# Loads of the rearranged Wo issued later, in a sliding-window attention block with a parallel gated MLP

## The chip, the cores and the metric

The kernel runs on one core of one Trainium2 chip. A core has a matrix engine (TensorE, PE in the profile; its weight loads stand apart as PEld), a vector engine (VectorE, DVE), a scalar engine (ScalarE, ACT), GpSimd (POOL) and SyncE (SP). In this kernel SP issues nearly all DMA transfers; 16 DMA engines carry them out. Each engine works through its own instructions in program order and waits on semaphores for the others. The metric is the device time of one execution in microseconds, lower is better. A run's time is the median over its executions; one more execution is recorded by the profiler, and all views of the profile are of that one.

## The reference

One layer for one prompt of S = 2048 positions of width D = 640: a layer norm, and from it, in parallel, a causal attention with a window of 256 positions (32 heads of 20) and a gated MLP of width 1536. All inputs are bfloat16.

```python
xn = layernorm(x)
qkv = xn @ wqkv                                # -> q, k, v: 32 heads of 20
scores = q @ k.T * 20 ** -0.5                  # per head
scores = where(0 <= i - j < 256, scores, -1e9)
attn = softmax(scores) @ v                     # heads side by side: 2048 x 640
g, u = xn @ w_gate, xn @ w_up
out = x + attn @ wo + (sigmoid(g) * u) @ w_down
```

## The kernel before

The positions are cut into four chunks of 512 (c = 0 to 3), each of four blocks of 128 rows. For each chunk TensorE computes q and k (`proj_block`, L266), v (`both_v`, L324; in chunk 0 L304), the twelve GLU blocks (`g_gu`: gate at L414, up at L423), the scores (`scores`, L500), the products with v (`pv`, L533) and the output (`g_out`). Around a GLU block ScalarE takes the tanh (L417) and VectorE makes h (L427). ScalarE takes the exponential of the scores (L506); GpSimd (L489) and VectorE (L517) set what lies outside the window to zero.

The output of a block of 128 rows is two PSUM tiles of 320 columns. In each, `down` (L437) sums h times w_down over 12 parts, and then `add_wo` (L444) adds attn times Wo over 5 parts. VectorE adds x, which lies in a tile `rows` (L448), and SP stores the result (L459). The rows of x are loaded by `new_rows` (L454), two blocks ahead at the start of `g_out`.

**Order.** The kernel is scheduled by hand: the order in which the program issues operations is the order on each engine. The main loop (L759) goes through steps of scores. Into the time of each step it pulls pieces of other work from a list, `fill`, whose parts stand in a fixed order (L726 to L745) with a cost in ns. A part with cost 0 is a group of DMA issues (`later`). The parts around the change are, in order: q and k of chunk 1 (`qk1`), the loads of w_down (`wd`), v of chunk 1 (`v1`), the rest of q and k of chunk 1 (`rest1`, issued by SP at L287), the loads of Wo (`wo`), the last three GLU blocks of chunk 0 (`gu0c`), the first two GLU blocks of chunk 1 (`gu1a`), and the output of chunk 0 with the third GLU block of chunk 1 inside its first block (`out0`). Beside `gu0c` and `gu1a` VectorE normalizes chunk 2 and turns it (`norm_block` L227, `turn_block` L244); when the last of four turns is done, SP writes it to DRAM (`turn_rows`, L249) and reads it back as xnT of chunk 2 (L251).

**Wo.** The rows of Wo are needed in another order than they have in DRAM. Eight DMAs that GpSimd issues beside q and k of chunk 1 (`turn_wo`, L179) write them in that order to a DRAM buffer `wo_i`. `load_wo` (L182) then loads them from there into the tile `wo`, 128 partitions of 5 x 640: four DMAs issued by SP, 32 partitions each, 200 KB each, in rows of 1280 bytes. The tile is written once and read in the outputs of all four chunks. A read of a tile waits for every write to the part that it reads, and a write for the writes of the same part before it.

In `g_out` the order of chunk 0 is: issue the two first `rows` loads; `down` for both halves of the first 128 rows; the third GLU block of chunk 1; then `add_wo` for both halves (the first use of Wo), `add_x`, and the store.

Of the kernel before, what the change touches and what calls it, by code (L numbers as in the profile page):

```python
# [69 lines left out]
def kernel(  # L70
# [11 lines left out]
    nc = tc.nc  # L82
# [42 lines left out]
    wo = const.tile([P, DC, D], BF16, name="wo")  # L125
# [54 lines left out]
                            in_=rows[r, side].rearrange("i (e w) -> e i w", e=16))  # L180

    def load_wo():  # L182
        for i in range(HG):
            nc.sync.dma_start(out=wo[32 * i:32 * i + 32, :, :],
                              in_=wo_i[i].rearrange("(m j) n -> j m n", j=32))
# [192 lines left out]
    def g_qk(c, behind={}):  # L378
        for w in "qk":
            for m in range(DC):  # L380
                proj_block(w, c, m)
                behind.get((w, m), lambda: None)()
                yield 5 * MM
        if c:
            spread("q", c, 0, 2)
            spread("k", c, 0, 2)
        else:
            for r in range(2):
                spread("q", c, r, r + 1)
                spread("k", c, r, r + 1)  # L390
                if r == 0:
                    load_gu(wu, B_w_up, 0, FS // 2)
# [13 lines left out]
    def part(w, d, f):  # L406
        k, first = divmod(f * P, FS)
        return w[k][:, d, first:first + P]

    def g_gu(c, f0, f1):  # L410
        for f in range(f0, f1):
            pg = ps_d.tile([P, CW], FP32, name="pg", tag="d")
            for d in range(DC):
                nc.tensor.matmul(pg, lhsT=part(wg, d, f), rhs=xnT[c][:, :, d, :],  # L414
                                 start=(d == 0), stop=(d == DC - 1))
            th = tp.tile([P, CW], FP32, name="th")
            nc.scalar.activation(out=th, in_=pg, func=TANH, scale=0.5)  # L417
            fill.hold = True
            yield 5 * MM
            fill.hold = False  # L420
            pu = ps_d.tile([P, CW], FP32, name="pu", tag="d")
            for d in range(DC):
                nc.tensor.matmul(pu, lhsT=part(wu, d, f), rhs=xnT[c][:, :, d, :],  # L423
                                 start=(d == 0), stop=(d == DC - 1))
            h = hp.tile([P, CW], BF16, name="h")
            ht[c, f] = h
            nc.vector.scalar_tensor_tensor(out=h, in0=th, scalar=1.0, in1=pu, op0=ADD, op1=MULT)  # L427
            yield 5 * MM
# [6 lines left out]
    def down(c, s, y, cut):  # L435
        for f in range(FC):
            nc.tensor.matmul(y[:, 0:cut[1] - cut[0]], lhsT=ht[c, f][:, s * P:(s + 1) * P],  # L437
                             rhs=wd[:, f, cut[0]:cut[1]], start=(f == 0), stop=False)
            if f % 6 == 5:
                yield 6 * 136  # L440
# [11 lines left out]
    def new_rows(c, s, name="rows", bufs=3, queue=nc.sync):  # L452
        rows = lnp.tile([P, D], BF16, name=name, bufs=bufs)
        queue.dma_start(out=rows, in_=xr[:, c * SBC + s, :])  # L454
        return rows
# [5 lines left out]
    def outp(c, s, ys, rows):  # L461
        for y, cut in zip(ys, HALVES):
            add_wo(c, s, y, cut)
        for y, cut in zip(ys, HALVES):
            add_x(y, cut, rows)
        store(c, s, rows)

    def g_out(c, between, ahead=()):
        coming = new_rows(c, 0)
        for s in range(SBC):  # L470
            rows = coming
            if s < SBC - 1:
                coming = new_rows(c, s + 1)
            if s == 0:
                yield from ahead
            ys = [ps_d.tile([P, CW], FP32, name=f"y{i}", tag="d") for i in range(2)]
            for y, cut in zip(ys, HALVES):
                yield from down(c, s, y, cut)
            if s == 0:
                yield from between  # L480
                fill.flush()
            outp(c, s, ys, rows)
            yield 10 * 136
# [128 lines left out]
    def mix(a, b, first, every=1, rest=True):  # L612

        for k, cost in enumerate(a):
            yield cost
            if k >= first and (k - first) % every == 0:
                yield next(b, 0)
        if rest:
            yield from b
# [94 lines left out]
    fill = Fill()  # L714
# [3 lines left out]
    def later(load, *args):  # L718
        load(*args)
        yield 0  # L720
# [8 lines left out]
    fill.add("wd", later(load_wd), 0)  # L729
    fill.add("v1", mix(g_v(1), norms2, 2, 1, False), 40 * 136)  # L730
    fill.add("rest1", later(spread_rest, 1), 0)
    fill.add("wo", later(load_wo), 0)
    fill.add("gu0c", mix(g_gu(0, 9, 12), norms2, 0, 1, False), 3 * GU)
    fill.add("gu1a", mix(g_gu(1, 0, 2), norms2, 0, 1, False), 2 * GU)
    fill.add("out0", mix(g_out(0, g_gu(1, 2, 3)), norms2, 1, 1), OUT + GU)
    fill.add("qk2", mix(g_qk(2), norms3, 2, 1, False), 50 * MM)
    fill.add("v2", g_v(2), 40 * 136)
# [108 lines left out]
```

## Time and profile before

| | us |
|---|---|
| median of 3 runs | 308.88 |
| lowest and highest of them | 308.87, 311.01 |
| the profiled execution, its own time | 309.65 |
| its span, from the first to the last instruction | 308.0 |
| ScalarE busy, VectorE busy | 193.2, 184.4 |
| GpSimd busy | 83.8 |

The span is 1.65 us shorter than the profiled execution's time; the rest lies around the program's instructions. The profiled execution is 0.77 us above the median. The granted clock of TensorE is 1.000 over the span.

DMA traffic is uneven. The page's 40 slices are 7.7 us each; their DMA share is 0.7 or more in most of the first eleven and lower, with peaks, after that:

```profile
DMA  7997739889927222721152113550000210000301
GB/s 213 347 306 238 266 102 309 220 248 320 198 94 199 85 72 93 228 80 47 43 128 72 39 65 99 163 192 2 3 2 2 70 41 23 2 2 2 88 21 64
```

The first line gives the mean busy share of the 16 DMA engines in tenths, the second what they moved. Two issues of Wo's neighbourhood, from the page's list (destination and source, queue, count, KB each, median us from issue to landing):

```profile
rows<-in_A_x_dram SPq DMA_DIRECT2D x12, 160.0 KB, 3.5
...
wo<-wo_i SPq DMA_DIRECT2D x4, 200.0 KB, 9.1
```

A landing time counts from the issue, so it holds the wait behind transfers that were issued before, as well as the transfer.

### The profile page before, as it was taken

Reading aid. Unit: us, or ns where it says so; the run is one execution under the profiler, and the core shown is the slowest. Engines: PE = TensorE matmul, PEld = TensorE weight load, DVE = VectorE, ACT = ScalarE, POOL = GpSimd, SP = SyncE. Lnnn points to the kernel's source line nnn. Section 1 sums busy time; section 2 is a strip of 40 time slices with the busy share of each in tenths; the row PEclk is TensorE's granted clock in tenths of the full one; section 3 lists DMA queues with packets and bytes.
Section 4 is the critical chain, followed back from the end, with each engine's and each line's share of the span. In section 5 each row is a group of like instructions: output and inputs, shape, how many; then the busy total and the mean of one; then the engine's idle time right before and its main releaser. Section 6 shows DMA issues by size and latency. Waiting matters only on the chain.

```text
span 308.0 us, 10147 instructions
## 1 busy us (share of the span) xinstructions
PE 302.9 (98%) x4431; PEld 168.2 (55%) x4431; DVE 184.4 (60%) x378; ACT 193.2 (63%) x183; POOL 83.8 (27%) x189
## 2 busy tenths in 40 slices
PE   7999999999999999999999999999999999999996
PEld 3654445564456655654456655644546765444774
DVE  5787449298984579577642666454383627465523
ACT  6923785977766458867655557777766466778000
POOL 5011234635314133422213122241314132221100
PEclk9999999999999999999999999999999999999999
DMA  7997739889927222721152113550000210000301
GB/s 213 347 306 238 266 102 309 220 248 320 198 94 199 85 72 93 228 80 47 43 128 72 39 65 99 163 192 2 3 2 2 70 41 23 2 2 2 88 21 64
DMA packets 35756, 36.86 MB, mean 120 GB/s; under 512 B 2944, under 2 KB 35456, under 8 KB 35712
## 3 DMA queue, kind: packets, MB, share of 16 engines
q1 hardware_dynamic: 34304, 33.84, 36.6%
q0 software_dynamic: 544, 1.61, 1.7%
q10 hardware_dynamic: 864, 0.77, 0.9%
q8 instruction: 34, 0.56, 0.8%
q14 instruction: 10, 0.08, 0.1%
HBM read 25.59 MB, written 11.44 MB: 120 GB/s over the span
## 4 chain that ended last, share of the span: by engine, by line
PE 97%; DMA 1%; ACT 1%; DVE 0%; issue 0%; SPq 0%
PE pg L414 18%; PE y L437 18%; PE pu L423 17%; PE pqk L266 15%; PE ps L500 9%; PE y L444 7%; PE acc L533 6%; PE pv L324 6%; PE pv L304 1%; DMA xc<-in_A_x_dram 1%; PE pvh L304 0%; PE pt L233 0%; ACT turn L640 0%; ACT turn L645 0%; DVE turn L651 0%
## 5 line engine op out<-in xcount | busy, mean ns | idle before, releaser
L506 ACT ACTIVATE pT<-ps 128x2048 bf16<-128x2048 f32 x75 | 140.8, 1877 | 56.0 <-PE ps L500 33.4
L489 POOL TENSOR_SCALAR_AFFINE_SELECT pT<-pT 64x256 bf16<-64x256 bf16 (+1 forms) x126 | 67.5, 536 | 181.0 <-ACT pT L506 122.9
L414 PE MATMUL pg<-xnT,wg 128*128 128x512 bf16 x240 | 59.9, 380 | 0.0
L423 PE MATMUL pu<-xnT,wu 128*128 128x512 bf16 x240 | 59.8, 380 | 0.0
L427 DVE SCALAR_TENSOR_TENSOR h<-th,pu 128x512 bf16<-128x512 f32 x48 | 32.9, 685 | 42.8 <-ACT th L417 25.7
L437 PE MATMUL y<-wd,h 128*128 128x320 bf16 (+2 forms) x396 | 56.8, 295 | 0.0
L266 PE MATMUL pqk<-xnT,wqkv 128*128 128x512 bf16 x200 | 45.8, 381 | 0.0
L437 PEld LDWEIGHTS <-h 128*128 128x128 bf16 x396 | 36.8, 98 | 15.9 <-issue 2.3
L517 DVE TENSOR_TENSOR pT<-pT,keep 128x512 bf16<-128x512 bf16 (+2 forms) x81 | 35.4, 444 | 15.6 <-ACT pT L506 14.7
L417 ACT ACTIVATE th<-pg 128x512 f32<-128x512 f32 x48 | 28.6, 595 | 20.2 <-PE pg L414 19.9
L423 PEld LDWEIGHTS <-wu 128*128 128x128 bf16 x240 | 22.3, 98 | 27.3 <-issue 2.2
L414 PEld LDWEIGHTS <-wg 128*128 128x128 bf16 x240 | 21.7, 98 | 26.4 <-issue 2.9
L266 PEld LDWEIGHTS <-wqkv 128*128 128x128 bf16 x200 | 22.6, 119 | 19.0 <-issue 1.5
L500 PE MATMUL ps<-qT,kT 20*64 20x320 bf16 (+4 forms) x1440 | 32.0, 260 | 0.0
L544 DVE STREAM_TRANSPOSE t<-acc 128x512 f32<-128x512 f32 x32 | 21.0, 694 | 17.9 <-PE acc L533 17.9
L448 DVE SCALAR_TENSOR_TENSOR rows<-y,rows 128x320 bf16<-128x320 f32 x30 | 14.4, 489 | 24.2 <-PE y L444 24.2
L500 PEld LDWEIGHTS <-kT 20*64 20x64 bf16 x1440 | 13.5, 103 | 27.2 <-issue 26.7
L444 PE MATMUL y<-wo,oc 128*128 128x320 bf16 (+2 forms) x165 | 24.2, 295 | 0.0
L533 PE MATMUL acc<-pT,v 64*32 64x320 bf16 (+4 forms) x1440 | 20.3, 253 | 0.5 <-issue 0.5
L533 PEld LDWEIGHTS <-v 64*32 64x32 bf16 x1440 | 17.0, 92 | 4.2 <-issue 1.6
L444 PEld LDWEIGHTS <-oc 128*128 128x128 bf16 x165 | 15.5, 98 | 6.7 <-issue 1.0
L324 PE MATMUL pv<-wqkv,xnT 128*64 128x320 bf16 x240 | 17.4, 300 | 0.0
(61 smaller groups left out, 173.3 us busy)
## 6 DMA issues: line engine op xcount, KB each, us to landing
qT<-sq SPq DMA_DIRECT2D x16, 256.0 KB, 4.2
kT<-sk SPq DMA_DIRECT2D x16, 256.0 KB, 4.3
xc<-in_A_x_dram SPq DMA_DIRECT2D x16, 160.0 KB, 4.0
sq<-st SPq DMA_DIRECT2D x20, 128.0 KB, 3.6
sk<-st SPq DMA_DIRECT2D x20, 128.0 KB, 2.9
out_dram<-rows SPq DMA_DIRECT2D x15, 160.0 KB, 1.8
wg<-in_B_w_gate_dram SPq DMA_DIRECT2D x4, 480.0 KB, 7.2
wu<-in_B_w_up_dram SPq DMA_DIRECT2D x4, 480.0 KB, 7.4
```

Of the source, the lines that this page charges most:

```text
L266: nc.tensor.matmul(ps, lhsT=wt[:, m, :], rhs=xnT[c][:, :, d, :], start=(d == 0), stop=(d == DC - 1))
L324: nc.tensor.matmul(ps[hf * U:(hf + 1) * U, 0:HALF], lhsT=xnT[c][:, s, d, rows], rhs=wqkv[:, d, 2 * D + hf * HALF:2 * D + (hf + 1) * HALF], ...
L414: nc.tensor.matmul(pg, lhsT=part(wg, d, f), rhs=xnT[c][:, :, d, :], start=(d == 0), stop=(d == DC - 1))
L423: nc.tensor.matmul(pu, lhsT=part(wu, d, f), rhs=xnT[c][:, :, d, :], start=(d == 0), stop=(d == DC - 1))
L427: nc.vector.scalar_tensor_tensor(out=h, in0=th, scalar=1.0, in1=pu, op0=ADD, op1=MULT)
L437: nc.tensor.matmul(y[:, 0:cut[1] - cut[0]], lhsT=ht[c, f][:, s * P:(s + 1) * P], rhs=wd[:, f, cut[0]:cut[1]], start=(f == 0), stop=False)
L444: nc.tensor.matmul(y[:, 0:cut[1] - cut[0]], lhsT=oc[c, m][:, s * P:(s + 1) * P], rhs=wo[:, m, cut[0]:cut[1]], start=False, stop=(m == DC - 1))
L489: nc.gpsimd.affine_select(out=part, in_=part, pattern=pattern, compare_op=GE, fill=0.0, base=-1 if sign > 0 else 0, channel_multiplier=sign)
L500: nc.tensor.matmul(ps[side * U:(side + 1) * U, i, col * U:(col + n) * U], lhsT=qk["k", kc, half][32 * i:32 * i + DH, 2 * r + side, kb * U: ...
L506: nc.scalar.activation(out=pt[:, :, 0:used, :], in_=ps[:, :, 0:used * U], func=EXP, scale=SCALE)
L517: nc.vector.tensor_tensor(out=part, in0=part, in1=limit.to_broadcast([P, HG, n * U]), op=MIN)
L533: nc.tensor.matmul(accs[side][32 * i:32 * i + 32, q * U:(q + n) * U], lhsT=vt[sb][rows, b, at:at + 32], rhs=pt[rows, i, col:col + n, :], s ...
```

## The change

Two lines. `load_wo` gets a VectorE memset that writes zero to the first element of `wo` in each of the 128 partitions, ahead of the four loads that overwrite it. So the first load, and with it all that SP issues behind it, waits until VectorE has come to that write. And the part `wo` of the list `fill` moves behind `gu0c` and `gu1a`, in front of `out0`, so that the write stands in VectorE's order behind the h of the second GLU block of chunk 1. SP's issues keep their order: between the old place and the new one no part issues anything on SP. Nothing that is computed changes.

```diff
     def load_wo():
+        nc.vector.memset(wo[:, 0, 0:1], 0.0)
         for i in range(HG):
             nc.sync.dma_start(out=wo[32 * i:32 * i + 32, :, :],
                               in_=wo_i[i].rearrange("(m j) n -> j m n", j=32))
...
     fill.add("v1", mix(g_v(1), norms2, 2, 1, False), 40 * 136)
     fill.add("rest1", later(spread_rest, 1), 0)
-    fill.add("wo", later(load_wo), 0)
     fill.add("gu0c", mix(g_gu(0, 9, 12), norms2, 0, 1, False), 3 * GU)
     fill.add("gu1a", mix(g_gu(1, 0, 2), norms2, 0, 1, False), 2 * GU)
+    fill.add("wo", later(load_wo), 0)
     fill.add("out0", mix(g_out(0, g_gu(1, 2, 3)), norms2, 1, 1), OUT + GU)
```

## The prediction, made before the changed kernel ran

> **What bounds the kernel now.** I read the busy table first, then the chain of waits in order of time around 70 to 98 us, then the timelines of SyncE's queue (SP) and of VectorE, then the landing times of the Wo loads, then stretches of DMA traffic.
>
> Busy table and, from the chain of waits in order of time (start us, us, what), the place where Wo is first used:
>
> ```profile
> PE 302.9 (98%) x4431; PEld 168.2 (55%) x4431; DVE 184.4 (60%) x378; ACT 193.2 (63%) x183; POOL 83.8 (27%) x189
> ...
> 81.09 0.86 PE acc L533 x54
> 81.94 0.55 issue
> 82.49 0.37 PE acc L533 x16
> ...
> 88.84 0.35 PE ps L500 x16
> 89.20 1.47 PE y L444 x10
> ```
>
> TensorE is busy 302.9 of 308.0 us and it works in program order, so a wait put into it is paid at the end, microsecond for microsecond, and at most about 5 us can be taken out. After the warm-up its only idle piece is the 0.55 us at 81.94, which no semaphore in the profile explains. L444 at 89.20 is the first matmul that reads Wo, and in the kernel before it is reached without a wait.
>
> Timeline of SP's queue (start us, us, engine, line), then the Wo loads' time from issue to landing:
>
> ```profile
> 71.59 1.03 SPq L287 DMA_DIRECT2D qT<-sq  x2
> 72.67 0.99 SPq L287 DMA_DIRECT2D kT<-sk  x2
> 74.61 2.94 SPq L184 DMA_DIRECT2D wo<-wo_i  x4
> 78.05 1.60 SPq L454 DMA_DIRECT2D rows<-in_A_x_dram  x2
> 89.02 0.38 SPq L249 DMA_DIRECT2D turn<-turn  x1
> ...
> DMA to landing us min/median/max: 8.9/9.1/9.4
> ```
>
> The four loads go out between 74.61 and 77.55 (the last instruction of the group starts at 77.2 and takes 0.3) and land 8.9 to 9.4 us after their issue, so the last is there at about 86.3: 2.8 us before L444.
>
> Timeline of VectorE:
>
> ```profile
> 82.11 0.67 DVE L427 SCALAR_TENSOR_TENSOR h<-th,pu 128x512 bf16<-128x512 f32 x1
> 82.70 0.41 DVE L517 TENSOR_TENSOR pT<-pT,keep 128x512 bf16<-128x512 bf16 x1
> 83.04 1.30 DVE L544 STREAM_TRANSPOSE t<-acc 128x512 f32<-128x512 f32 x2
> 84.27 0.80 DVE L244 STREAM_TRANSPOSE turn<-xc 128x640 bf16<-128x640 bf16 x1
> 85.00 0.30 DVE L554 RECIPROCAL rec<-t 128x32 f32<-128x32 f32 x1
> ```
>
> The h at 82.11 is that of the second GLU block of chunk 1. VectorE has no idle time in these lines; its pace here is its own, not TensorE's.
>
> Stretches (us, then busy by engine, granted clock, DMA share, GB/s):
>
> ```profile
> 74.00:78.00 4.00, 4.00 (x41) 1.67 (x39) 3.35 (x9) 3.07 (x4) 1.60 (x4) 1.00 1.08 356
> 78.00:83.00 5.00, 4.45 (x125) 2.29 (x125) 5.00 (x10) 4.53 (x4) 1.84 (x4) 1.00 1.10 197
> 94.90:96.90 2.00, 2.00 (x16) 1.29 (x14) 1.11 (x3) 1.84 (x1) 0.71 (x2) 1.00 0.93 243
> ```
>
> The engines are full (share about 1) in all three, but what they move differs: 356 GB/s with wd, qT and kT in front, 197 with Wo and rows, 243 with the 32-partition loads of xc. From 86 on the DMA engines stand still until 89.9.
>
> **The change, part by part.** The added write is one VectorE memset of 128x1. The only such write in the trace (L374) took 59 ns. In the changed program's order it stands behind the third L244 of the chunk and in front of the reciprocal of L554, not straight behind the h of the second block, since the masks, the acc transposes and one turn come between. L244 ends at 84.27 + 0.80 = 85.07, the write at about 85.13. Its 59 ns delay what VectorE does next; the last of it that L444 needs is oc, done at 87.44 of the timeline, 1.7 us ahead, so this costs nothing.
>
> The wait: the first Wo load now waits in SP for that write. SP answers a VectorE end quickly (L249 is issued at 89.02, its L244 ended at 89.00), so the first load goes out at 85.15 instead of 74.61. Loads that wait for nothing else go out every 0.46 us (four xc loads in 1.85 us), so the four start at 85.15, 85.61, 86.07 and 86.53. Behind them in SP are the two row loads (from 78.05 to about 87.0 and 87.5) and the turn of chunk 2 at 89.02, which is behind its own L244 anyhow and is not moved. Its xnT is first used at 108.44, more than 8 us after it lands.
>
> Landing: the 9.1 us of before are queueing behind 1 MB of qT and kT and 2 MB of wd. At 85 that is gone. A 160 KB load into an empty system (rows at 101.07) took 2.2 us; 200 KB should take 2.3, so the first Wo load lands at 87.45. The other three follow at the rate of the engines. For 204.8 kB each I take 243 GB/s, the row of loads of the same kind (32 partitions, 1280-byte rows), nearest in shape: 0.84 us each, so the last lands at 87.45 + 3 x 0.84 = 89.97. Against TensorE's 89.13 for the first Wo matmul (its start on the timeline), that is a stall of **0.85 us**. Bounds: at 356 GB/s it lands at 87.45 + 3 x 0.575 = 89.18, no stall to speak of; if the rate is no limit, the issue is, 86.53 + 2.2 = 88.7, 0.4 us early. At 197 GB/s for Wo and rows together (1147 kB in 5.8 us, first packet 0.9 us after issue as for the turn at 89.02) all is there at 91.9, a stall of 2.75 us. The weights for L444 need all four loads, so the last one decides.
>
> The 197 of before came with these very loads, and 356 with 128-partition ones. The Trainium skill, "DMA: Bandwidth & Descriptors", section Anatomy of one DMA, prices a transfer at about 2.0 us plus its bytes over 436 GB/s (fitted for transfers issued by GpSimd): for 819 kB from 85.15 an estimate of 89.0, no stall. No row here reaches 436, so I give the case its own smaller chance below.
>
> The rows: the first lands some 0.4 us behind the last Wo load, and the add at L448 needs it 0.9 us after L444 starts. They move together and cost nothing more. If they land 1 us later still, VectorE waits, and TensorE does not need the freed PSUM pair before the acc at 97.38.
>
> What is removed: the traffic of Wo in 78 to 86. The 0.55 us at 81.94 lies in it and may be instruction records that came late (queue 8 has one 16 KB packet there, 1.7% of 16 engines over 5 us, so 1.4 us long). But between 66 and 72 such a packet took 2.7% of 6 us, 2.6 us, with no stall. So it may go or stay, worth -0.55 to 0. If it goes, TensorE reaches L444 at 88.58 and waits there for the same landing: the gain is swallowed. It counts only where the loads are early.
>
> Sum: +0.85 us at L444, 0 elsewhere. On the profiled execution 309.65 + 0.85 = 310.5; the median of the runs is 0.77 below it, 308.88, so I predict **309.7**.
>
> **The rivals.**
>
> *Hidden, and slightly faster.* The idle engines drain each load as fast as it is issued, the last lands at 88.7, before the 89.13, and the stall at 81.94 is gone with the traffic. For it: nothing else moves from 86 to 89.9. Against: the rate of 197 just where Wo was moving. TensorE then waits only from 88.58 to 88.7, and the time is 308.88 - 0.4 = 308.5; it is 308.9 if the gap stays. It decides from about 366 GB/s on (204.8 kB in (89.13 - 87.45) / 3 = 0.56 us).
>
> *Slow landing, slower by over 1%.* The long landing is the loads' own (32 partitions each, 160 short rows, source in DRAM), not the queue's. At 8.9 us from issue the last lands at 86.53 + 8.9 = 95.4, a stall of 6.3 us: 315.2. It passes 1% from a landing of 5.7 us on, since 92.2 is 3.1 us past 89.13. For it: even the last Wo load, with the queue emptying, took 8.9. Against: xnT and xc of the same pattern landed in a median of 3.4 and 4.2. A gap so long may cost more: the ten opening matmuls of L199 run in 4.36 us, 0.44 each, where five of L414 take 1.08, 0.22 each, so a cold stretch of that length loses about 2.2 us: 317.4. The Trainium skill, "TensorE: Matmul & The Clock Gate", Part 1, has the clock halve after an idle window of about 3.4 us. The trace grants 1.00 throughout, also in the stretch with the 0.55 us gap, so no run here shows it.
>
> *Nothing moves.* The write would have to come out early, so that the loads go out about when they did: 308.9. The program's order speaks against it.
>
> **How the numbers follow.** Forecast 0.67, hidden 0.15, slow landing 0.13, nothing moves 0.03, and 0.02 for a gain I have no mechanism for. The time is the forecast's, 309.7. The range goes from the hidden case, 308.5, to the upper bound of the forecast, 308.88 + 2.75 = 311.6; it leaves out the slow landing and the unknown gain, 0.15. About 1% (3.1 us) is what a measurement of this kernel can tell from no change. Faster by that 0.02, slower 0.13 (the slow landing), within it 0.85.
>
> **What would show it.** In the changed profile: a 128x1 memset on VectorE at 85.1; Wo loads on SP from 85.15 to about 86.9; the landing down from 9.1 to 3 to 4 us; TensorE's wait before L444 on the Wo loads, 0.3 to 2.7 us; and no other new wait on TensorE. With no wait there and no gap at 82, the hidden case holds. A landing above 5.7 us would prove the forecast wrong, as would a stall that stands in another place (rows, xnT of chunk 2) or loads issued much before or after 85.

## The result and the profile after

| | before | after |
|---|---|---|
| median of 6 runs each, us | 309.0 (308.83 to 311.01) | 313.36 (311.78 to 314.77) |
| the profiled execution, us | 309.65 | 313.4 |
| its span, us | 308.0 | 311.7 |
| its mean granted clock | 1.000 | 0.995 |

The ratio is 1.0123, 95% interval 1.0095 to 1.0152: the changed kernel is slower by 1.2%. The medians lie 4.4 us apart, the profiled spans 3.7. The prediction was 309.7, with 311.6 as its upper end. Medians here are over all executions, while ratios leave out those more than 1.5% above the fastest of the same kernel: 770.66 and 508.8 us in the second of the shorter holds below, 322.26 in the kernel with another order of the loads, and one of 610.28 of the kernel before.

VectorE's timeline of the changed kernel (start us, us, engine, line, operation):

```profile
84.30 0.79 DVE L245 STREAM_TRANSPOSE turn<-xc 128x640 bf16<-128x640 bf16 x1
85.04 0.34 DVE L555 RECIPROCAL rec<-t 128x32 f32<-128x32 f32 x1
85.05 0.06 DVE L183 MEMSET wo<- 128x1 bf16 x1
```

SP's timeline of it:

```profile
85.14 1.76 SPq L185 DMA_DIRECT2D wo<-wo_i  x4
86.94 0.91 SPq L455 DMA_DIRECT2D rows<-in_A_x_dram  x2
89.09 0.38 SPq L250 DMA_DIRECT2D turn<-turn  x1
```

And the landing of its Wo loads:

```profile
DMA to landing us min/median/max: 2.9/3.8/4.6
```

The write comes at 85.05, the loads leave from 85.14 in place of 74.61, and the turn of chunk 2 leaves when it did before (89.02). The landing has shrunk from about 9 us to 2.9 for the first load and 4.65 for the last. That last load was issued at 86.47, as the next but one view shows, and the sum of the two is 91.1.

What the DMA engines moved from 85 us to that landing, and the loads issued in this time (KB each, median us to landing):

```profile
DMA packets 1004, 1.17 MB, mean 192 GB/s; under 512 B 89, under 2 KB 1004, under 8 KB 1004
...
wo<-wo_i SPq DMA_DIRECT2D x4, 200.0 KB, 3.8
turn<-turn SPq DMA_DIRECT2D x1, 640.0 KB, 4.3
rows<-in_A_x_dram SPq DMA_DIRECT2D x2, 160.0 KB, 4.4
```

The four loads of Wo are 0.82 MB. So 0.35 MB more had moved before the last of them was there: data of the two rows loads (0.33 MB in all) and of the turn, which SP issued behind Wo.

From its chain of waits in order of time (start us, us, what):

```profile
86.47 4.65 DMA wo<-wo_i
91.11 0.09 issue
91.20 2.78 PE y L445 x10
93.98 1.23 PE y L438 x6
95.21 0.36 PE ps L501 x24
95.57 2.55 PE y L438 x18
```

TensorE's waits (who waited for whom, us, times, longest):

```profile
PE y L445 <- DMA wo<-wo_i: 2.8, 1, 2.8
```

L445 is L444 of before. TensorE waits 2.8 us for Wo, once, and starts the product at 91.20 where the kernel before started it at 89.13. The gap of 0.55 us at 81.94 is gone from the list of waits, and no other new wait stands in it. But the ten matmuls that follow take 2.78 us on the chain (1.47 before) and the next six 1.23 (0.81 before). They are the same instructions. Stretches (us, then busy by engine, granted clock, DMA share, GB/s) show why:

```profile
86.00:88.00 2.00, 2.00 (x13) 0.75 (x11) 2.00 (x5) 1.59 (x2) 0.00 (x0) 1.00 0.99 230
88.00:90.00 2.00, 0.42 (x17) 0.14 (x16) 1.97 (x4) 1.45 (x1) 0.00 (x0) 1.00 1.02 211
90.00:92.00 2.00, 0.80 (x4) 0.52 (x5) 0.00 (x0) 0.42 (x1) 0.92 (x2) 0.82 1.08 318
92.00:94.00 2.00, 2.00 (x9) 1.12 (x8) 0.49 (x1) 0.00 (x0) 0.00 (x0) 0.50 0.39 142
94.00:96.00 2.00, 2.00 (x34) 1.13 (x33) 0.82 (x2) 0.35 (x1) 0.00 (x0) 0.83 0.76 189
```

The granted clock is 0.50 right behind the wait and back at 1.00 before 96. What it lost over the three stretches is 2 x (0.18 + 0.50 + 0.17) = 1.7 us. Finer stretches give the edges:

```profile
87.87:91.28 3.41, 0.62 (x18) 0.26 (x18) 2.10 (x4) 1.88 (x1) 0.72 (x2) 1.00 1.07 235
91.28:94.69 3.41, 3.41 (x14) 1.94 (x14) 1.16 (x3) 0.00 (x0) 0.20 (x1) 0.50 0.52 175
```

The clock is at half for 3.41 us, and in the 3.41 us ahead of that TensorE was busy for 0.62 and idle for 2.79.

So the 3.73 us (the product of w_down with 18 matmuls starts at 95.50 on TensorE's timeline, 91.77 before) have two terms. L444 starts **2.07 us** late, and the halved clock then costs **1.66 us**. Of the 2.8 us of waiting 0.72 were won before it, since TensorE came to the place at 88.41; 0.55 of that is the gap.

The six runs show the second term by themselves. All have the same program. One has a clock of 1.000 and a span of 310.1, four have 0.995 and 311.4 to 311.8, one has 0.988 and 313.1. A mean of 0.995 over 311.7 us is a loss of 1.6 us, which is what lies between the first and the four. The run that kept its clock is 2.1 us above the profiled span of before: the wait alone.

The medians are 0.7 us further apart than the profiles. The profiled execution of before took 309.65 us, but three of its six executions took 308.83 to 308.88, 0.8 us less, while after the change the profiled execution is at the median. The profile of before has the gap of 0.55 us at 81.94. If the executions at 308.8 do not have it, all 2.8 us of the wait count against them, and 2.8 + 1.6 is the 4.4 of the medians. No trace shows such an execution, so this is not shown; the profiles of the two shorter holds below, which have neither gap nor wait, have spans of 307.5 and 307.2, which fits.

### The profile page after: what moved, and what is told of

Read it like the earlier page. It is cut to its first block, busy times and chain, and to the rows that moved or that the text cites. A ratio compares the mean times of both kernels' runs of the same rounds, so it can differ in the third digit from the quotient of the medians.

```text
span 311.7 us, 10150 instructions
## 1 busy us (share of the span) xinstructions
PE 304.7 (98%) x4431; PEld 169.1 (54%) x4431; DVE 184.4 (59%) x379; ACT 193.1 (62%) x183; POOL 83.4 (27%) x189
## 4 chain that ended last, share of the span: by engine, by line
PE 92%; DVE 3%; DMA 2%; ACT 1%; SPq 0%; issue 0%; DVEq 0%
PE y L438 16%; PE pg L415 16%; PE pu L424 16%; PE pqk L267 14%; PE ps L501 8%; PE y L445 8%; PE acc L534 6%; PE pv L325 5%; DMA wo<-wo_i 1%; PE pv L305 1%; DMA xc<-in_A_x_dram 1%; DVE turn L245 1%; DVE h L428 1%; PE pvh L305 0%; DVE t L545 0%
## 5 line engine op out<-in xcount | busy, mean ns | idle before, releaser
L445 PE MATMUL y<-wo,oc 128*128 128x320 bf16 (+2 forms) x165 | 25.5, 305 | 2.8 <-DMA wo<-wo_i 2.8
L445 PEld LDWEIGHTS <-oc 128*128 128x128 bf16 x165 | 15.9, 100 | 10.1 <-issue 3.8
```

The lines of the kernel that those rows point to most:

```text
L445: nc.tensor.matmul(y[:, 0:cut[1] - cut[0]], lhsT=oc[c, m][:, s * P:(s + 1) * P], rhs=wo[:, m, cut[0]:cut[1]], start=False, stop=(m == DC - 1))
```

## The experiments

The theory after this reading: the loss is the wait at L444 for the last Wo load, and behind it a clock that the wait brings down. Three questions are tested: is it the hold, or the new place in the list, or what stands behind it on SP; does the clock follow the wait; and why does the last load land as late as 91.1. Each kernel was timed against the kernel before.

**The move without the write.**

```diff
     def load_wo():
-        nc.vector.memset(wo[:, 0, 0:1], 0.0)
         for i in range(HG):
```

> The part stays behind the GLU blocks in the list, the VectorE write is taken out, so nothing holds SP. Theory (the wait for the late loads is the loss): SP's order is the same as before, the loads go out at 74 to 78 us, no wait at L444 and a granted clock of 1.000; time 309.0, within 0.5 us of before, and the 0.55 us gap on TensorE near 82 is back or within the spread. Rival (the new place in the list costs, by moving work on some engine): about 313, as the changed kernel.

Measured: 309.47 against 309.3, ratio 1.0002 (0.9982 to 1.0022). SP's timeline:

```profile
74.19 2.94 SPq L184 DMA_DIRECT2D wo<-wo_i  x4
```

TensorE's waits, without those of the opening:

```profile
PE acc L533 <- issue: 0.6, 1, 0.6
```

The loads leave when they did before, the gap near 82 is back, and the loss is gone. The place in the list by itself does nothing; the write holds the loads.

**Half of the loads held.**

```diff
+    fill.add("wo0", later(load_wo, 0, 2), 0)      # loads 0 and 1, no write
     fill.add("gu0c", ...)
     fill.add("gu1a", ...)
-    fill.add("wo", later(load_wo), 0)
+    fill.add("wo1", later(load_wo, 2, HG), 0)     # the write to partitions 64 to 127, loads 2 and 3
```

> Loads 0 and 1 of Wo go out at the old place, loads 2 and 3 wait for the write. Theory (the last landing decides): two held loads leave at 85.1 and 85.5 and land as the first two of the changed kernel did, by 88.9; TensorE reaches L444 at 88.4 and waits 0.3 to 0.6 us, clock 1.000; 308.7 to 309.3. Rival (SP standing still from 74 to 85, with rows and the turn of chunk 2 queued behind, is what costs): the hold is the same, so 311 to 313.

Measured: 309.82, ratio 1.0019 (1.0004 to 1.0033); clock 1.000. SP stood still just as long, until 85.2, and the loss is a seventh of the changed kernel's. TensorE's waits, without the opening:

```profile
PE y L446 <- DVE turn L246: 0.6, 1, 0.6
```

The issues of 85 to 86 us with their median landing, the two held loads:

```profile
wo<-wo_i SPq DMA_DIRECT2D x2, 200.0 KB, 3.3
```

The wait's line names a turn of VectorE, which TensorE does not need here. (In the second of the shorter holds below, the same product starts at 88.37, inside that turn.) It had to have the Wo loads, issued at 85.2 and 85.6; the second landed at 89.22, and TensorE started at 89.32, as far behind the landing as in the changed kernel (91.11 and 91.20). The hold of SP costs nothing; the last landing decides. What the engines moved from 85 us to that landing:

```profile
DMA packets 611, 0.71 MB, mean 169 GB/s; under 512 B 55, under 2 KB 611, under 8 KB 611
```

The two held loads are 0.41 MB; the other 0.30 are nearly all of the two rows loads, which SP issued behind them from 86.06 on. The time is 0.5 us above the expectation's upper end, partly from a landing 0.3 us later than the 88.9 taken from the changed kernel.

**TensorE kept busy in the wait.**

```diff
                 fill.flush()
+            if c == 0 and s == 0:
+                for _ in range(24):
+                    nc.tensor.matmul(ys[0][:, HALF:CW], lhsT=ones[:, 0:P], rhs=ones[:, 0:CW - HALF],
+                                     start=False, stop=False, skip_group_check=True)
             outp(c, s, ys, rows)
```

> The changed kernel with 24 more matmuls of 128x192 on TensorE just ahead of the first L444; they write PSUM columns that nobody reads and take about 2.4 us of the 2.8 us wait. Theory (two terms: L444 2.0 us late, and 1.7 us from a halved clock that the idle time brings on): no idle time above 0.5 us, clock 1.000, so 2.0 to 2.2 us above before, 311.0 to 311.3. Rival (the clock falls for another reason, or the 1.7 us are not the clock's): 313 or more, since 24 matmuls are added. Clock below 1 with the wait filled would disprove the theory.

Measured: 312.43, ratio 1.0099 (1.0065 to 1.0134), profiled span 310.4, clock 1.000. TensorE's timeline:

```profile
88.68 2.22 PE L485 MATMUL y<-const-bfloat16-1.0 128*128 128x192 bf16 x24
91.49 1.52 PE L445 MATMUL y<-wo,oc 128*128 128x320 bf16 x10 [0.58 <-issue]
```

The product with Wo starts as late as in the changed kernel, but takes 1.52 us, not 2.78. With 24 matmuls more, the profiled execution is 1.3 us shorter. So the filled wait keeps the clock, and the profile's loss is the 2.4 us that L445 starts late (91.49 against 89.13). All four executions of this kernel are on record with a clock of 0.999 or 1.000, against one of six of the changed kernel (the trace itself holds no clock record; the 1.52 us of the ten matmuls are those of before). The median is 1.1 us above the expected range, and the clock is not the reason. The expectation counted 2.0 to 2.2 us from the median of 309.0; the profile counts its 2.4 from an execution of 309.65, and the median is another 0.3 above the profiled 312.16.

**A hold 2.8 us longer.** `load_wo`, with its write, stands behind the first `down` of the first block of chunk 0; the rows loads go ahead of it on SP.

```diff
                 yield from down(c, s, y, cut)
+                if c == 0 and s == 0 and cut == HALVES[0]:
+                    load_wo()
...
-    fill.add("wo", later(load_wo), 0)
```

> The write and the loads stand behind the first half of the first w_down product, so the write comes at 87.8 in place of 85.05, 2.8 us later; the two rows loads go ahead of Wo. Theory: last landing 4.65 us after an issue at 89.2, at 93.9; TensorE waits 5.4 us and L444 starts 4.8 us later than before; with the same clock loss of 1.6 to 3.0 us 315.4 to 316.8. Rival A (the clock loss grows with the wait, 0.6 us per us): about 317.2. Rival B (landing is faster with the rows out of the way, last load 3.4 us after issue): L444 at 92.7, 314.1 to 315.5.

Measured: 316.8, ratio 1.0235 (1.0200 to 1.0270). TensorE's timeline:

```profile
94.19 2.83 PE L445 MATMUL y<-wo,oc 128*128 128x320 bf16 x10 [5.76 <-DMA wo<-wo_i]
```

The landing of its Wo loads:

```profile
DMA to landing us min/median/max: 2.8/4.0/4.9
```

Stretches, the granted clock third from the end:

```profile
90.00:94.00 4.00, 0.00 (x0) 0.00 (x0) 0.00 (x0) 0.43 (x1) 0.92 (x2) 0.65 1.01 254
94.00:98.00 4.00, 3.81 (x15) 2.17 (x16) 1.31 (x3) 0.00 (x0) 0.00 (x0) 0.50 0.46 134
98.00:102.00 4.00, 4.00 (x65) 2.37 (x64) 0.42 (x1) 2.12 (x2) 1.18 (x2) 1.00 1.07 229
```

L445 starts at 94.19, 5.06 us later than before, and the clock is at half until 98: (98.0 - 94.19) / 2 = 1.9 us more, 6.96 in all, where the span grew by 6.9. The half clock before 94 fell into idle time and cost nothing, so by the profile the loss from the clock did not grow with the wait (the interval of the time does not exclude rival A's 317.2). Rival B expected a faster landing with the rows out of the way, and the last load still needs 4.9 us. But that does not settle whether the loads behind Wo slow it, because another one took their place: the turn of chunk 2, issued at 89.73. What the engines moved from 87.8 us to the last landing at 94.05:

```profile
DMA packets 1102, 1.32 MB, mean 212 GB/s; under 512 B 68, under 2 KB 1102, under 8 KB 1102
```

That is 0.50 MB more than Wo.

**Shorter holds.** In one kernel the held part stands between `gu0c` and `gu1a`, in the other between the two GLU blocks of `gu1a`.

```diff
     fill.add("gu0c", ...)
+    fill.add("gu1x", mix(g_gu(1, 0, 1), norms2, 0, 1, False), GU)   # second kernel only
+    fill.add("wo", later(load_wo), 0)
     fill.add("gu1a", ...)                         # second kernel: g_gu(1, 1, 2), GU
-    fill.add("wo", later(load_wo), 0)
```

> The held part stands behind the last GLU blocks of chunk 0 and ahead of those of chunk 1; the write comes at about 78.6, behind the second turn of VectorE. Theory: loads out from 78.6 to 80.0, into engines that have just run empty (in the changed kernel their traffic ends at 79), last landing at about 84.6, 4 us ahead of L444; no wait, clock 1.000. If the 0.55 us gap near 82 came from the traffic of Wo it may stay, since Wo now moves from 79.5 to 84: 308.5 to 309.0. Rival (any hold costs): above 309.5.

> The held part stands between the first and the second GLU block of chunk 1; the write comes at about 81.85. Theory: loads out from 81.9 to 83.3, last landing 4.65 us later at 87.9, 0.5 us ahead of TensorE at L444 (88.4); no wait, or one of under 0.3 us, clock 1.000; the gap near 82 is gone as in the changed kernel, so 308.4 to 308.8, the smallest of all. Rival (landing slower, 5.2 us and more): a wait up to 0.5 us, 309.0.

Measured: 309.22, ratio 1.0012 (0.9994 to 1.0030), and 309.13, ratio 0.9995 (0.9982 to 1.0007). The profiled spans are 307.5 and 307.2 against 308.0; neither has a wait at L445 nor a gap near 82. Both medians lie 0.2 to 0.3 us above the expected ranges; the kernel before took 309.27 beside them, 0.3 above the 309.0 of the result. The last landing of the first kernel came at 86.9, not at 84.6, still 1.8 us ahead of its use at 88.7. The second kernel is at the edge. Its loads and landings:

```profile
L185 SPq DMA_DIRECT2D wo<-wo_i x4: 321/432/1162, 82.0 to 84.0; - x4
DMA to landing us min/median/max: 3.6/4.1/4.5
```

TensorE's timeline of the same kernel:

```profile
88.02 0.42 PE L501 MATMUL ps<-qT,kT 20*64 20x320 bf16 x16
88.37 1.40 PE L445 MATMUL y<-wo,oc 128*128 128x320 bf16 x9
```

The last load, issued at 84.0, is there at 88.3, and TensorE needs it at 88.4. A hold that ends 3 us earlier is free. The half microsecond and more that the profiled spans gain does not show in the intervals, so no version here is shown to beat the kernel before. In the first kernel Wo moves between 80 and 87 and the gap near 82 is gone all the same, so traffic of Wo at that moment is not enough to explain the gap. What causes it stays open.

**Why the last load lands late: source and shape.** Two kernels read Wo in its own row order, with the same hold; the rearrangement is left out of what they compute.

```diff
-                              in_=wo_i[i].rearrange("(m j) n -> j m n", j=32))
+                              in_=A_wo.rearrange("(m i j) n -> i j m n", i=HG, j=32)[i])
...
+        for m in range(DC):                     # second kernel, in place of the loop over i
+            nc.sync.dma_start(out=wo[:, m, :], in_=A_wo[m * P:(m + 1) * P, :])
```

> The held loads read Wo itself in place of its rearranged copy, again four loads of 32 partitions with rows of 1280 bytes; the rearrangement is left out of the computation. Control for the next run: if the source does not matter, last landing at 91.1, wait 2.8 us, time 313 as the changed kernel. Rival (the rearranged copy in DRAM reads slowly): landing at 89 to 89.5, time 309 to 309.5.

> As the run before, but five loads of 128 partitions and 160 KB each, the same 819 kB in rows of 1280 bytes, and the same hold; the rearrangement is left out. Theory (32 partitions per load are what keeps the rate at 200 GB/s): at 356 GB/s the issue limits, 87.0 + 2.2 = 89.2 for the last; wait 0.8 us, L444 at 89.3, clock 1.000, time 309.0 to 309.4. Rival (the rate is that of any held load): last landing at 91, 313.

Measured: 313.31, ratio 1.0120 (1.0094 to 1.0145), for 32 partitions; 310.31, ratio 1.0030 (1.0014 to 1.0047), for 128, 0.9 us above the expected range. TensorE's wait for Wo, first in the first kernel, then in the second:

```profile
PE y L445 <- DMA wo<-in_A_wo_dram: 3.2, 1, 3.2
PE y L444 <- DMA wo<-in_A_wo_dram: 0.6, 2, 0.4
```

The Wo loads of the second, from first to last start, and their landing:

```profile
L185 SPq DMA_DIRECT2D wo<-in_A_wo_dram x5: 352/430/432, 85.4 to 87.2; - x5
DMA to landing us min/median/max: 2.3/3.1/3.2
```

The rearranged copy is not what is slow: read from Wo itself, the last load lands at 91.6, 0.5 us later than in the changed kernel, and the time is the same. The shape of the loads is part of it. The last of the five lands at 87.2 + 3.2 = 90.4 at most, at least 0.7 us earlier than in the changed kernel though issued 0.8 us later, but not at the 89.2 that 356 GB/s would give. From 88 to 90 us the engines moved 275 GB/s, and 211 in the changed kernel. The rest of the gain has another reason: each of the five matmuls of a product needs one of these loads, so TensorE starts with the first ones and waits 0.6 us in two pieces.

**First reading, and the order of the partitions.**

```diff
+    fill.add("wo0", later(load_wo, False), 0)     # first kernel: all four once more, not held, ahead of wd
     fill.add("wd", later(load_wd), 0)
...
-        for i in range(HG):
+        for i in (0, 2, 1, 3):                    # second kernel
```

> The changed kernel, and the same four loads once more without the hold, ahead of w_down's loads, at about 66 us; the held ones at 85.1 write the same data again. What is still open is why four loads take until 91.1. Theory A (what is read for the first time comes slowly, as w_down did at 69 to 71 us with 180 to 200 GB/s and then 385): the held loads read again what was read before and land at 87.4, 87.9, 88.5 and 89.2; wait under 0.9 us, clock 1.000, 309.0 to 309.8. Theory B (the rate belongs to the loads' pattern, whatever was read before): landings as in the changed kernel, the last at 91.1, 312 to 313.5. In both, w_down lands 2.5 us later than before, at about 80, 2 us ahead of its first use.

> The changed kernel with the four loads in the order 0, 2, 1, 3, so that loads that follow each other write partitions of different halves (0 to 63, 64 to 127). Theory (two loads in a row into the same half get in each other's way): the pairs 0, 1 and 2, 3 are taken apart, last landing 0.5 to 1.5 us earlier, at 89.6 to 90.6, wait 1.2 to 2.2 us, 310 to 312.5. Rival (each load is slow by itself, or the reading side sets the rate): last landing at 91.1, 313.3.

Measured: 313.97, ratio 1.0172 (1.0145 to 1.0199), and 314.25, ratio 1.0141 (1.0101 to 1.0182). In both TensorE waits 2.8 us for Wo and the longest landing of a held load is 4.6 us. Reading the data a second time does not help, nor does the order: both theories fall. But these two profiles are of value in another way. TensorE's timeline of the first:

```profile
91.31 1.52 PE L446 MATMUL y<-wo,oc 128*128 128x320 bf16 x10 [2.78 <-DMA wo<-wo_i]
92.67 0.98 PE L439 MATMUL y<-wd,h 128*128 128x320 bf16 x6
```

The same wait as in the changed kernel, 2.78 us, and this time the ten matmuls take 1.52 us. The granted clock is 1.000 in both, and the spans are 310.4 and 310.3, where the changed kernel's profile has 311.7. A wait of this length brings the clock down in some executions and not in others. Of the 18 executions with all four loads held until 85 us (the changed kernel, the control with 32 partitions and these two), four kept 1.000 and took 311.77 to 312.21 us, eleven have 0.995, and three have less, one of them 0.945 at 322.26 us.

What decides is how the wait falls, as far as these traces show. In the traces that record the clock, its changes from one end to the other lie a whole number of 3.413 us apart: 85.33 us, 25 of them, between the first two in the changed kernel; 307.2 us, 90 of them, here. Counted on from the first change of this trace at 4.31 us, edges stand at 86.23, 89.64 and 93.06, and the wait lies across one of them:

```profile
86.23:89.64 3.41, 2.30 (x26) 0.84 (x23) 3.41 (x7) 2.45 (x3) 0.00 (x0) 1.00 1.00 236
89.64:93.06 3.42, 1.75 (x13) 1.30 (x14) 1.14 (x4) 0.90 (x1) 0.92 (x2) 1.00 0.93 291
```

TensorE is idle for 1.1 us of the first stretch and 1.7 of the second; in the other profile it is 1.3 and 1.5. In the three profiles where the clock fell behind the wait (the changed kernel, the longer hold, the control), TensorE was idle for 2.7 to 2.8 us of the 3.41 us just ahead of the fall. Around this wait, then, 2.7 us idle within one stretch halved the clock in the next, and 1.7 us did not. Nothing between the two was measured there.

## Why the prediction was wrong

**Right, by the profile:** where the write lands (85.13 said, 85.05 measured); that the loads leave from 85.15; that landing becomes short once qT, kT and w_down are out of the way; that the only new wait is TensorE's before L444; that nothing waits for the rows or the turn of chunk 2; that the gap at 82, if it goes, is swallowed. That SP's standing still costs nothing in itself was also shown by runs: half of the loads held, with SP stopped as long, costs 0.6 us by its ratio, and TensorE's wait for Wo accounts for that.

**The landing was mis-sized.** The step said 2.3 us for the first load and 0.84 us for each further one, last landing 89.97. Measured: 2.9 us for the first, and last landing 91.11, so (91.11 - 88.04) / 3 = 1.02 us each, which is 200 GB/s. The engines were not that slow: 230 and 211 GB/s in the stretches from 86 to 90, not far from the 243 of the step. What it had wrong is the amount. It gave the engines to Wo's 0.82 MB alone and let the rows land behind; but 1.17 MB had moved by the last landing of Wo, and in the half-held kernel 0.71 MB where the Wo loads were 0.41. The slow bound had the right picture, Wo and rows together, all there at 91.9. That the last rows load landed at 91.8 is partly luck: the bound had neither the higher rate nor the turn's share. This is read from the amounts moved: no run holds the loads with nothing behind them, so the price of the loads beside them alone is not measured. A second reading, the order of the loads and the rearranged copy as the source are not the cause; the shape counts for something.

Together the landing is 1.14 us later than said, and L444 started 2.07 us late, not 0.85. By the profile this alone comes to 309.0 + 2.07 = 311.1, within the range. By the times it does not: the four executions with this hold and a full clock took 311.77 to 312.21, 0.2 to 0.6 us above the range's end. The prediction took 0.77 us off the profiled execution to come to the median, in the changed kernel as well, and there the two are the same (313.4 and 313.36). The Trainium skill, "DMA: Bandwidth & Descriptors", Anatomy of one DMA, gave an estimate of 89.0 for the last landing; measured, it is 91.1, with the rows and the turn moving beside the loads, so the measurement decides against it for four loads of this shape in this place.

**The clock was left out.** This is the step that put the time well outside the range. The prediction had the clock fall only in the slow rival, behind a wait of 6.3 us, and let the forecast's own bound of 2.75 us stand without it. The runs show a loss of about 1.6 us in four of six executions, none in one, about twice as much in one; in the profile it stands right behind a wait of 2.8 us. Filling the wait takes it away, in all four executions of that kernel. The Trainium skill, "TensorE: Matmul & The Clock Gate", Part 1, says that the window in which idleness is judged is about 3.4 us long and runs on its own, not in step with the kernel. The traces agree: the clock's changes lie multiples of 3.413 us apart, and the two profiles with the same wait and a full clock have it split between two stretches. Where the page is read as a threshold (gaps over 3.4 us), the trace differs, and decides: 2.8 us was enough when it fell into one stretch.

**The rivals.** None came true as written. The slow rival had the clock fall behind the wait at L444, which happened, but behind a landing as long as before, 8.9 us, which did not. It was to pass 1% from a landing of 5.7 us; with the clock's 1.7 us added, 4.65 us did. The hidden case is what the shorter hold shows: with the last landing at 88.3 there is no wait and no loss.

## What to carry to other kernels

A load that is moved next to its use needs slack for the last landing of its whole group, and the amount to divide by the rate is all that moves at that time, with the loads issued right behind the group. On a TensorE-bound kernel a wait of a few microseconds has a second price behind it, the clock, and the upper end of a range must hold both. When such a wait can't be avoided, let each matmul wait for its own part of the data, which here left 0.6 us of waiting, or give TensorE something to do, which here kept the clock.

## What the hardware showed that I had not expected

A wait of 2.8 us on TensorE led to a granted clock of 0.50 for 3.41 us (1.7 us lost), yet the same wait in the same place left it at 1.000 in one run of the changed kernel and in two other profiles, where an edge of the 3.413 us grid on which the clock changes cut the wait into 1.1 and 1.7 us, and 1.3 and 1.5. And a group of loads did not have the engines to itself for having been issued first: when the last of the four Wo loads was there, the engines had moved 1.17 MB, where the group has 0.82, since loads issued behind it moved beside it.
